# A decode kernel that streams a key and value cache: four accumulated products, other cuts of the loads, no marking loads

## The chip, the cores and the metric

The kernel runs on one core of a Trainium2 chip. A core has five engines that run side by side: TensorE (PE, matrix products into PSUM), VectorE (DVE), ScalarE (ACT), GpSimd (POOL) and SyncE (SP, which here only issues transfers). Sixteen DMA engines move data between HBM and the on-chip memory SBUF. The metric is the device time of one execution in microseconds.

## The reference

Two blocks share a normalised input and are added to it. Block A is one decode step of attention with 32 heads, 4 batches and a cache of 4096 positions of 128 numbers. Block B is a small gated unit (a projection to 1728, GELU, a layer norm of one half, a gate, a projection back to 640). In essence:

```
xn = layernorm(x)                               # x is (4, 1, 640)
q = (xn @ wq) as (4, 32, 1, 128)
p = softmax(q . k_cache * 128 ** -0.5)          # k_cache, v_cache: (4, 32, 4096, 128), bf16
A = (p . v_cache) as (4, 1, 4096) @ wo          # wo is (4096, 640)
z = gelu(xn @ w_in); z1, z2 = halves of z; z2 = layernorm(z2)
out = x + A + (z1 * (w_sp * z2 + b_sp)) @ w_out
```

Nearly all bytes are the two caches, 134 MB each, and each is read once.

## The kernel before

**Units.** The 32 heads are taken in four groups of eight (`g`), and within a group the four batches (`b`) one after another. A unit is the K or the V cache of one group and batch: 128 partitions by 64 KB, 8 MB. There are 16 K units (K0 to K15) and 16 V units; unit number u is group u // 4, batch u % 4. A partition holds 256 positions of one head, 16 partitions make a head.

**Order.** `seq` (L153) is K0, K1, K2, K3, then V0, K4, V1, K5 and so on to V11, K15, then V12 to V15. The main loop (L553) first issues the load of the next unit on SP's queue and then emits the work of the present one. SP's queue is served in order, so a load that waits holds back those behind it. A framework adds the waits between engines and may place instructions of one engine in another order than the text.

**Slots.** `kv` (L94) has five slots of 32 KB in each partition, and a unit takes two. `place` (L159 to L166) says which: V units lie in slots 0 and 1, even K units in 3 and 4, odd ones in 2 and 3 (there are other places at the start; V13 lies in 2 and 3, V15 in 3 and 4). A load waits until what lay in its slots has been consumed. `cuts` (L167) lists units that are loaded in pieces: K3, K7, K11 and K15 (the last of each group) in two halves, and V15 as 192 and 64 of its 256 positions. `first` (L169) lists K units of which the second half is consumed first: the odd ones from u = 4 that are not cut (K5, K9, K13). That half of an odd unit lies in slot 3, which the next unit needs.

**A K unit** (`emit_K`, L409) is eight steps: DVE transposes a piece (L417), PE multiplies it with q into the scores S (L428). After the last unit of a group, `softmax` (L469) finds the largest score (L435 to L445), takes the exponential on ACT (L473), transposes it on DVE (L479) and spreads it (`z_fill`, L448) over ACT, DVE and POOL into two buffers of weights, for batches 0 and 1.

**A V unit** (`emit_V`, L492) is 64 products (L500) into O. DVE masks and sums O into R (L509, L510; for V15 in four steps, L512 and L514). For batches 0 and 1, `z_fill` for the batch two later follows.

**The heads of a group.** `emit_sel` and `emit_oT` turn R (partitions by batch by 128 numbers) into rows of oT, the stationary operand of the last projection. One f32 product with SelX spreads the heads over 32 rows (L523), where every row holds all four quarters of its head's 128 numbers. DVE masks the quarter that belongs to the row (L526), adds the four (L537) and multiplies by the inverse row sum (L538). For groups one to three this stands inside the last K unit of the next group, for group four at the end.

**The end.** `load_wo` (L193) loads wo into slots 0 and 1 (40 KB in each partition, 32 columns of 640) in pieces of 16, 11, 4 and 1 columns. The products of columns 0 to 15 (L546; CL is 16) are added to `proj` in PSUM, which already holds x and block B; DVE copies and adds its halves (L587, L591) while PE does columns 16 to 31 into `last`. L601 adds both and two transfers write the result.

**The start.** wq, w_in, pieces of w_out and K0 are loaded; POOL and DVE build constant masks (SelX among them, L259) and block B is computed while K0 and K1 arrive. Six small loads into the tile `walk` (L557 to L559) follow on SP's queue; nothing reads them. They are the marking loads: each has its own size and row count, by which it can be told in a list of transfers.

Of the kernel before, what the change touches and what calls it, by code (L numbers as in the profile page):

```python
# [9 lines left out]
ALU = mybir.AluOpType  # L10
AX = mybir.AxisListType
F32 = mybir.dt.float32
BF16 = mybir.dt.bfloat16
# [3 lines left out]
def kernel(  # L17
# [19 lines left out]
    nc = tc.nc  # L37
    P = 128
    B, Sq, D = A_x.shape
# [3 lines left out]
    HG = 8  # L43
# [3 lines left out]
    T = Sk // M  # L47
# [5 lines left out]
    NU = NG * B  # L53
# [21 lines left out]
    const = ctx.enter_context(tc.tile_pool(name="const", bufs=1))  # L75
    small = ctx.enter_context(tc.tile_pool(name="small", bufs=2))

    NKT = 2 * TC * 32
    ppool = ctx.enter_context(tc.tile_pool(name="ppool", bufs=2))
# [8 lines left out]
    def misc_ps(shape, dtype):  # L88
        misc_ctr[0] += 1
        return ps_m.tile(shape, dtype, tag="misc", name=f"misc{misc_ctr[0]}")  # L90
# [38 lines left out]
    w_in = at_slot(2, n_in).rearrange("p (c f) -> p c f", c=DC)  # L129
    nc.sync.dma_start(out=w_in, in_=B_w_in.rearrange("(p c) f -> p c f", c=DC))  # L130

    walk = const.tile([8, 286], BF16)
    sw = nc.gpsimd.dma_start(out=walk[:, 0:128], in_=B_w_out[0:8, 0:128].rearrange("(r i) n -> i r n", i=4))
    MS = 15 * NOUT // 2
    nc.vector.memset(w_words[:, 0:MS], 0.0)
    nc.gpsimd.memset(w_words[:, MS:FC * NOUT // 2], 0.0)
# [2 lines left out]
    def load_piece(eng, t):  # L139
        p0, p1, st, c0, n, k, run = PC[t]  # L140
        return eng.dma_start(out=w_out[p0:p1:st, c0:c0 + n].rearrange("p c n -> p (c n)"),
                             in_=B_w_out[f_of[t][0]:f_of[t][1], :].rearrange("(r i c) n -> i r (c n)", i=k, c=run))
# [3 lines left out]
    for t in ("w", "s", "n", "m", "l"):  # L146
        with tc.issue_after(sw.ins):
            sw = load_piece(nc.gpsimd, t)
# [10 lines left out]
    place = {("k", 0): (3, 4), ("k", 1): (0, 1), ("k", 2): (2, 3), ("k", 3): (4, 0)}  # L159
# [2 lines left out]
    for u in range(NU):  # L162
        place[("v", u)] = (0, 1)
    place[("v", 0)] = (1, 2)
    place[("v", NU - 3)] = (2, 3)
    place[("v", NU - 1)] = (3, 4)  # L166
    cuts = {("k", u): (0, T // 2, T) for u in range(NU) if u % B == B - 1}  # L167
    cuts[("v", NU - 1)] = (0, 192, T)
    first = {u: u % 2 for u in range(B, NU) if ("k", u) not in cuts}  # L169

# [18 lines left out]
    CW = H * Dh // P  # L189
    RQ = Dh // CW  # L190
    wo_t = at_slot(0, CW * NOUT).rearrange("p (c n) -> p c n", c=CW)

    def load_wo(c_cuts):  # L193
        for c0, c1 in zip(c_cuts[:-1], c_cuts[1:]):
            nc.sync.dma_start(out=wo_t[:, c0:c1, :], in_=A_wo.rearrange("(p c) n -> p c n", c=CW)[:, c0:c1, :])
# [55 lines left out]
    SelH = const.tile([P, HG], F32)  # L251
    i2 = SelP[:].rearrange("p (h c) -> p c h", c=2)
    nc.gpsimd.tensor_tensor(out=SelH[:], in0=i2[:, 0], in1=i2[:, 1], op=ALU.add)
    Mk4 = const.tile([P, 4], F32)
# [1 line left out]
    nc.gpsimd.tensor_tensor(out=h4[:, 0:16], in0=I32[:, 0:16], in1=I32[:, 16:32], op=ALU.add)  # L256
    nc.gpsimd.tensor_tensor(out=h4[:, 16:24], in0=h4[:, 0:8], in1=h4[:, 8:16], op=ALU.add)
    nc.gpsimd.tensor_tensor(out=Mk4[:], in0=h4[:, 16:20], in1=h4[:, 20:24], op=ALU.add)
    SelX = const.tile([P, HG, RQ], F32)  # L259
    nc.gpsimd.tensor_copy(out=SelX[:], in_=SelH[:, :, None].to_broadcast((P, HG, RQ)))  # L260
    MkB = const.tile([P, B], F32)
    b8 = const.tile([P, 8 + HP], F32)
    nc.gpsimd.tensor_tensor(out=b8[:, 0:8], in0=SelP[:, 0:8], in1=SelP[:, 8:16], op=ALU.add)
# [5 lines left out]
    for q in range(4):  # L269
        nc.gpsimd.tensor_copy(out=SelE[32 * q:32 * q + 32, :, q % 2, :],  # L270
                              in_=b8[32 * q:32 * q + 32, 8:8 + HP, None].to_broadcast((32, HP, RQ)))
# [10 lines left out]
                          in_=ident_f[:].rearrange("p (q x c) -> p q x c", q=2, c=C2))  # L282
# [4 lines left out]
    for hf in range(NH):  # L287
        nc.tensor.matmul(proj[0:32, 0:NO2], lhsT=ident_bf[:XR, 1 - hf:33 - hf],  # L288
                         rhs=x_bf[:, hf * NO2:(hf + 1) * NO2], start=(hf == 0), stop=False)
# [4 lines left out]
    for hf in range(2):  # L294
        for c in range(DC):
            for j in range(NG):
                n0 = j * HG * Dh + hf * 512
                nc.tensor.matmul(q4_ps[32 * j:32 * j + 32, hf * 512:hf * 512 + 512], lhsT=xnT[:, c, :],  # L298
                                 rhs=wq[:, c, n0:n0 + 512], start=(c == 0), stop=(c == DC - 1))
# [4 lines left out]
    for a in range(2):  # L304
        op = nc.vector.tensor_copy if a == 0 else nc.scalar.copy
# [34 lines left out]
    for c in range(DC):  # L340
        for parts in z_parts:
            for j, (dst, src) in enumerate(parts):
                nc.tensor.matmul(dst, lhsT=xnT[:, c, :], rhs=src[:, c], start=(c == 0 and j == 0),  # L343
                                 stop=(c == DC - 1 and j == len(parts) - 1))
# [4 lines left out]
    for (bk, q, t), (col, m, n, c0, x0, x1, st) in z_at_col.items():  # L349
        rows = slice(32 * q, 32 * q + 32)  # L350
        nc.scalar.activation(out=zT[rows, :, c0:c0 + n, x0:x1:st],  # L351
                             in_=zr_ps[bk][rows, :, col:col + m].rearrange("p a (x c) -> p a c x", c=n),
# [37 lines left out]
    for f0 in range(0, FC, 4):  # L390
        for hf in range(NH):
            for fc in range(f0, min(f0 + 4, FC)):
                nb = 32 if fc == 1 and hf == 0 else RW
                u0, r0 = 32 * fc + 1 - hf, 32 * (fc % 2)
                nc.tensor.matmul(proj[r0:r0 + nb, 0:NO2], lhsT=uT[:, u0:u0 + nb],  # L395
                                 rhs=w_out[:, fc, hf * NO2:(hf + 1) * NO2],
                                 start=(fc == 1 and hf == 0), stop=False)
# [9 lines left out]
    state = {}  # L407
# [110 lines left out]

    def emit_sel(g):

        ox = misc_ps([P, B, RQ, CW], F32)
        r0 = 32 * g
        nc.tensor.matmul(ox[r0:r0 + 32].rearrange("p b q c -> p (b q c)"), lhsT=SelX[:].rearrange("p h q -> p (h q)"),  # L523
                         rhs=state["R"][:].rearrange("p b d -> p (b d)"), start=True, stop=True)
        om = ppool.tile([P, B, RQ, CW], F32, tag="p", name="om")
        nc.vector.tensor_tensor(out=om[r0:r0 + 32], in0=ox[r0:r0 + 32],  # L526
                                in1=Mk4[r0:r0 + 32, None, :, None].to_broadcast((32, B, RQ, CW)), op=ALU.mult)
        state[("om", g)] = om

    oT = const.tile([P, CW * RW + 32], BF16)  # L530
    nc.gpsimd.memset(oT[:], 0.0)

    def emit_oT(g):
        r0 = 32 * g
        om = state.pop(("om", g))
        oR = small.tile([P, B, CW], F32, tag="oR", bufs=1)
        nc.vector.tensor_reduce(out=oR[r0:r0 + 32], in_=om[r0:r0 + 32].rearrange("p b q c -> p b c q"), axis=AX.X, op=ALU.add)  # L537
        nc.vector.tensor_tensor(out=oT[r0:r0 + 32, 1:1 + CW * RW].rearrange("p (c b h) -> p c b h", c=CW, h=NH)[:, :, :, 0],  # L538
                                in0=oR[r0:r0 + 32].rearrange("p b c -> p c b"),
                                in1=state.pop(("rinv", g))[r0:r0 + 32, None, :].to_broadcast((32, CW, B)), op=ALU.mult)  # L540

    def o_mul(dst, c, hf, n0, n1, start, stop):
# [10 lines left out]
    for i, item in enumerate(seq):  # L553
        if i + 1 < len(seq):
            key, u = seq[i + 1]
            load_unit(seq[i + 1])
            if i == 0:  # L557
                for k, m0, m in ((1, 128, 72), (2, 200, 56), (8, 256, 24), (1, 280, 2), (1, 282, 2), (1, 284, 2)):
                    nc.sync.dma_start(out=walk[0:k, m0:m0 + m], in_=B_w_out[0:k, 0:m])  # L559
        else:  # L560
            load_wo((0, 16, 27, 31, 32))
        key, u = item
        g, b = divmod(u, B)
        if key == "k":
            done = b == B - 1 and g > 0
            for k in range(8):
                emit_K(u, k)
                if done and k == 1:
                    emit_sel(g - 1)
                if done and k == 2:  # L570
                    emit_oT(g - 1)
            if b == B - 1:
                if g < NG - 1:
                    fill_qz(g + 1)
                softmax(g)
        else:
            emit_V(u)
    emit_sel(NG - 1)
    emit_oT(NG - 1)

    CL = 16
    for c in range(0, CL, 2):
        for hf in range(NH):
            for p in range(2):
                o_mul(proj[32 * p:32 * p + 32], c + p, hf, hf * NO2, (hf + 1) * NO2, False, c == CL - 2 and hf == NH - 1)
    o_1 = ppool.tile([32, NO2], F32, tag="p", name="o_1")
# [3 lines left out]
    for k in range(2):  # L590
        nc.vector.tensor_tensor(out=o_q[32 * k:32 * k + 32, :], in0=proj[32:64, k * NQ:(k + 1) * NQ],  # L591
                                in1=o_1[:, k * NQ:(k + 1) * NQ], op=ALU.add)
    last = ps_l.tile([64, NQ], F32)
    for c in range(CL, CW):
        for hf in range(NH):
            for k in range(2):
                n0 = hf * NO2 + k * NQ
                o_mul(last[32 * k:32 * k + 32], c, hf, n0, n0 + NQ, c == CL and hf == 0, c == CW - 1 and hf == NH - 1)

# [33 lines left out]
```

## Time and profile before

| what | value |
|---|---|
| median of three runs | 663.61 us (662.76 to 663.67) |
| the profiled execution | 663.03 us |
| its span (first to last instruction) | 661.1 us |
| HBM read | 282.25 MB, 427 GB/s over the span |
| DVE busy | 378.3 us, 57% (283.0 of it the transposes of L417) |
| PE busy | 286.1 us, 43% |
| ACT, POOL busy | 74.7 and 76.6 us |
| the chain that ended last | DMA 72%, issue 12%, DVE 10%, PE 4% |

The profile is that of one execution. It gives the busy time of each engine, the busy share in 40 slices (a digit 9 is 90% or more), the chain of work that ended last (at each step, what released it), and a timeline: start, duration, engine, line, operation, output and input, how many, and in brackets the idle time before and what ended it. The span is 1.9 us shorter than the time of the same execution. A line L417 is a line of the kernel before.

### The profile page before, as it was taken

The numbers are of one execution on the slowest core, as the hardware profiler recorded it, in microseconds if no ns is written. First come the engines' busy times: TensorE is split into PE (matmuls) and PEld (weight loads), VectorE is DVE, ScalarE is ACT, GpSimd is POOL, SyncE is SP. The second block draws the span as 40 slices with busy tenths as digits, with TensorE's granted clock in tenths as the row PEclk, the third lists the DMA queues.
The fourth block names the chain that finished last, engine by engine and source line by source line (L and its number), as shares of the span: only waits on it lengthen the run. The fifth ranks groups of instructions, "written<-read, shape, count | busy, mean of one in ns | idle before, by whom it ended". The sixth has DMA issues, their size and how long they took to land.

```text
span 661.1 us, 5628 instructions
## 1 busy us (share of the span) xinstructions
PE 286.1 (43%) x2345; PEld 107.8 (16%) x2345; DVE 378.3 (57%) x312; ACT 74.7 (11%) x144; POOL 76.6 (12%) x135
## 2 busy tenths in 40 slices
PE   0436556336062546315335165533517065632145
PEld 0222212112021111101112021111202021111013
DVE  4239999756191759719164377756537195870112
ACT  0310000331100000430200000060200000061100
POOL 7440000031200000030300000030300000021200
PEclk9858888769578596667768587766857667865678
DMA  9999999999999999999999999999999999999997
GB/s 368 446 447 433 409 445 424 444 441 428 429 428 433 444 407 450 425 433 440 441 416 433 432 420 453 440 417 441 421 436 440 437 428 415 434 438 436 420 423 297
DMA packets 6686, 282.60 MB, mean 427 GB/s; under 512 B 1096, under 2 KB 1232, under 8 KB 1364
## 3 DMA queue, kind: packets, MB, share of 16 engines
q1 hardware_dynamic: 6266, 281.60, 98.8%
q0 software_dynamic: 368, 0.65, 0.3%
q8 instruction: 18, 0.29, 0.2%
q14 instruction: 6, 0.05, 0.0%
q10 hardware_dynamic: 28, 0.01, 0.0%
HBM read 282.25 MB, written 0.01 MB: 427 GB/s over the span
## 4 chain that ended last, share of the span: by engine, by line
DMA 72%; issue 12%; DVE 10%; PE 4%; POOL 1%; ACT 1%; SPq 0%; DVEq 0%; POOLq 0%; ACTq 0%
DMA kv<-in_A_k_cache_dram 54%; DMA kv<-in_A_v_cache_dram 10%; DVE w_words L417 10%; DMA kv<-in_A_wo_dram 4%; DMA kv<-in_B_w_in_dram 4%; PE O L500 2%; PE proj L395 1%; POOL kv L379 0%; PE misc L343 0%; PE S L428 0%; PE last L546 0%; ACT kv L351 0%; POOL z_b L381 0%; POOL kv L364 0%; ACT L351 0%
## 5 line engine op out<-in xcount | busy, mean ns | idle before, releaser
L417 DVE STREAM_TRANSPOSE w_words<-kv 128x2048 f32<-128x2048 f32 x128 | 283.0, 2276 | 118.3 <-DMA kv<-in_A_k_cache_dram 115.8
L428 PE MATMUL S<-w_words,QZ 128*32 128x512 bf16 x1024 | 183.9, 491 | 253.8 <-DVE w_words L417 253.8
L428 PEld LDWEIGHTS <-QZ 128*32 128x32 bf16 x1024 | 59.2, 109 | 377.7 <-issue 312.9
L500 PE MATMUL O<-kv,w_words 128*32 128x512 bf16 x1024 | 74.8, 457 | 55.7 <-DMA kv<-in_A_v_cache_dram 48.2
L465 ACT ACTIVATE w_words<-w_words,MkE 32x128 bf16<-32x128 bf16 x120 | 60.8, 507 | 115.0 <-PE O L500 101.9
L509 DVE TENSOR_TENSOR om<-O,Mk 128x512 f32<-128x512 f32 x15 | 10.4, 692 | 91.0 <-PE O L500 91.0
L463 POOL TENSOR_SCALAR w_words<-w_words,MkE 32x128 bf16<-32x128 bf16 x60 | 43.1, 719 | 136.3 <-PE O L500 115.3
L500 PEld LDWEIGHTS <-w_words 128*32 128x32 bf16 x1024 | 33.8, 112 | 96.6 <-issue 65.6
L473 ACT ACTIVATE w_words<-S,negmax 128x1024 bf16<-128x1024 f32 x4 | 4.5, 1114 | 396.6 <-DVE negmax L445 396.6
L403 POOL COPY QZ<-qT 32x32 bf16<-32x32 bf16 x16 | 5.1, 317 | 268.0 <-PE S L428 267.5
L461 DVE TENSOR_SCALAR w_words<-w_words,MkE 32x128 bf16<-32x128 bf16 x76 | 24.9, 327 | 2.4
L510 DVE TENSOR_REDUCE R<-om 128x128 f32<-128x512 f32 x15 | 15.3, 1019 | 0.5
L484 POOL TENSOR_SCALAR rs<-MkB,rowsum 128x4 f32<-128x4 f32 x4 | 1.2, 299 | 112.7 <-ACT w_words L473 112.7
L479 DVE STREAM_TRANSPOSE w_words<-w_words 128x1024 bf16<-128x1024 bf16 (+1 forms) x8 | 9.6, 1241 | 5.9 <-ACT w_words L473 5.9
L395 PE MATMUL proj<-w_words,z_b 128*8 128x320 bf16 (+1 forms) x52 | 5.9, 411 | 8.8 <-DVE z_b L382 8.8
L512 DVE TENSOR_SCALAR R<-O,Mk 128x128 f32<-128x128 f32 x1 | 0.4, 352 | 14.0 <-PE O L500 14.0
L435 DVE TENSOR_REDUCE m<-S 128x1 f32<-128x1024 f32 x4 | 4.9, 1225 | 5.6 <-PE S L428 5.6
L523 PE MATMUL misc<-R,SelX 128*32 128x512 f32 x8 | 4.2, 604 | 7.2 <-DVE R L510 5.5
L298 PE MATMUL q<-kv,xnT 128*32 128x512 bf16 x40 | 4.1, 590 | 6.2 <-DVE xnT L228 6.2
L487 PE MATMUL misc<-rs,SelE 128*32 128x4 f32 x8 | 1.1, 205 | 10.7 <-POOL rs L484 10.7
L288 PE MATMUL proj<-kv,ident_bf 8*32 8x320 bf16 x2 | 0.7, 445 | 10.8 <-DMA kv<-in_A_x_dram 10.8
L526 DVE TENSOR_TENSOR om<-misc,Mk 32x512 f32<-32x512 f32 x4 | 2.7, 687 | 4.5 <-PE misc L523 4.5
(101 smaller groups left out, 92.9 us busy)
## 6 DMA issues: line engine op xcount, KB each, us to landing
kv<-in_A_k_cache_dram SPq DMA_DIRECT2D x8, 4096.0 KB, 29.8
kv<-in_A_v_cache_dram SPq DMA_DIRECT2D x1, 6144.0 KB
kv<-in_A_wq_dram SPq DMA_DIRECT2D x1, 5120.0 KB
kv<-in_A_wo_dram SPq DMA_DIRECT2D x1, 2560.0 KB
kv<-in_B_w_in_dram SPq DMA_DIRECT2D x1, 2160.0 KB, 23.7
kv<-in_A_v_cache_dram SPq DMA_DIRECT2D x1, 2048.0 KB
kv<-in_A_wo_dram SPq DMA_DIRECT2D x1, 1760.0 KB
kv<-in_A_wo_dram SPq DMA_DIRECT2D x1, 640.0 KB, 26.7
```

Source lines behind the costliest of these rows:

```text
L395: nc.tensor.matmul(proj[r0:r0 + nb, 0:NO2], lhsT=uT[:, u0:u0 + nb], rhs=w_out[:, fc, hf * NO2:(hf + 1) * NO2], start=(fc == 1 and hf == 0) ...
L403: nc.gpsimd.tensor_copy(out=QZ[r0:r0 + 32, :, :, :, 8 + 8 * hp], in_=qT[32 * g:32 * g + 32, NE * hp:NE * hp + NE].rearrange("p e a b -> p ...
L417: nc.vector.transpose(kT.rearrange("p (t r) -> p t r", r=32), kw)
L428: nc.tensor.matmul(S_ps[32 * q:32 * q + 32, i], lhsT=QZ[:, b, 2 * kh + w, e, w0:w0 + 32], rhs=kb[:, i, :, e, :, w], start=(b == 0 and k < ...
L435: nc.vector.tensor_reduce(out=m1[:], in_=S_ps[:].rearrange("p i t m -> p (i t m)"), axis=AX.X, op=ALU.max)
L461: nc.vector.tensor_scalar(out=dst, in0=src, scalar1=mk, scalar2=None, op0=ALU.mult)
L463: nc.gpsimd.tensor_scalar(out=dst, in0=src, scalar1=mk, scalar2=None, op0=ALU.mult)
L465: nc.scalar.activation(out=dst, in_=src, func=ACT.Copy, scale=mk)
L479: nc.vector.transpose(pT_t[:, j0:j1, :], blocks)
L500: nc.tensor.matmul(O_ps[32 * q:32 * q + 32, :, :], lhsT=Zb[b % 2][:, w].rearrange("p h c -> p (h c)"), rhs=vv[:, w * 4 * Dh:(w + 1) * 4 * ...
L509: nc.vector.tensor_tensor(out=om4[:], in0=O_ps[:], in1=Mk4[:, :, None].to_broadcast((P, 4, Dh)), op=ALU.mult)
L510: nc.vector.tensor_reduce(out=R, in_=om4[:].rearrange("p c d -> p d c"), axis=AX.X, op=ALU.add)
```

## The change

- `emit_sel` makes four accumulated products instead of one. SelX becomes four blocks, one for each quarter d of the 128 numbers; block d sends head h to the row of quarter d alone. The sum of the four products is what L526 and L537 made on DVE, and these two go.
- wo is loaded in pieces of 12, 8, 8, 3 and 1 columns, and columns 0 to 19 go into `proj` (CL is 20).
- K7, K11 and K15 are loaded whole; K3 alone stays in two halves. By the rule of `first`, their second halves are then consumed first.
- V13 lies in slots 3 and 4, V15 in 2 and 3.
- The six marking loads go, and `walk` shrinks to what the one GpSimd load needs.

```diff
-    walk = const.tile([8, 286], BF16)
+    walk = const.tile([8, 128], BF16)
...
-    place[("v", NU - 3)] = (2, 3)
-    place[("v", NU - 1)] = (3, 4)
-    cuts = {("k", u): (0, T // 2, T) for u in range(NU) if u % B == B - 1}
+    place[("v", NU - 3)] = (3, 4)
+    place[("v", NU - 1)] = (2, 3)
+    cuts = {("k", B - 1): (0, T // 2, T)}
...
-    SelX = const.tile([P, HG, RQ], F32)
-    nc.gpsimd.tensor_copy(out=SelX[:], in_=SelH[:, :, None].to_broadcast((P, HG, RQ)))
+    SelX = const.tile([P, RQ, HG * RQ], F32)
+    nc.gpsimd.memset(SelX[:].rearrange("p d r -> p (d r)"), 0.0)
+    sx = SelX[:]
+    nc.gpsimd.tensor_copy(out=bass.AP(sx.tensor, sx.offset, [list(sx.ap[0]), [HG * RQ + 1, RQ], [RQ, HG]]),
+                          in_=SelH[:, None, :].to_broadcast((P, RQ, HG)))
...
-        ox = misc_ps([P, B, RQ, CW], F32)
+        ox = misc_ps([P, B, CW], F32)
         r0 = 32 * g
-        nc.tensor.matmul(ox[r0:r0 + 32].rearrange("p b q c -> p (b q c)"), lhsT=SelX[:].rearrange("p h q -> p (h q)"),
-                         rhs=state["R"][:].rearrange("p b d -> p (b d)"), start=True, stop=True)
-        om = ppool.tile([P, B, RQ, CW], F32, tag="p", name="om")
-        nc.vector.tensor_tensor(out=om[r0:r0 + 32], in0=ox[r0:r0 + 32],
-                                in1=Mk4[r0:r0 + 32, None, :, None].to_broadcast((32, B, RQ, CW)), op=ALU.mult)
-        state[("om", g)] = om
+        for d in range(RQ):
+            nc.tensor.matmul(ox[r0:r0 + 32], lhsT=SelX[:, d], rhs=state["R"][:, :, d * CW:(d + 1) * CW],
+                             start=(d == 0), stop=(d == RQ - 1))
+        state[("ox", g)] = ox
...
-        om = state.pop(("om", g))
-        oR = small.tile([P, B, CW], F32, tag="oR", bufs=1)
-        nc.vector.tensor_reduce(out=oR[r0:r0 + 32], in_=om[r0:r0 + 32].rearrange("p b q c -> p b c q"), axis=AX.X, op=ALU.add)
         nc.vector.tensor_tensor(out=oT[r0:r0 + 32, 1:1 + CW * RW].rearrange("p (c b h) -> p c b h", c=CW, h=NH)[:, :, :, 0],
-                                in0=oR[r0:r0 + 32].rearrange("p b c -> p c b"),
+                                in0=state.pop(("ox", g))[r0:r0 + 32].rearrange("p b c -> p c b"),
                                 in1=state.pop(("rinv", g))[r0:r0 + 32, None, :].to_broadcast((32, CW, B)), op=ALU.mult)
...
-            if i == 0:
-                for k, m0, m in ((1, 128, 72), (2, 200, 56), (8, 256, 24), (1, 280, 2), (1, 282, 2), (1, 284, 2)):
-                    nc.sync.dma_start(out=walk[0:k, m0:m0 + m], in_=B_w_out[0:k, 0:m])
         else:
-            load_wo((0, 16, 27, 31, 32))
+            load_wo((0, 12, 20, 28, 31, 32))
...
-    CL = 16
+    CL = 20
```

More of the change, by code (lines that the diff above doesn't have):

```diff
@@ L130 @@
     nc.sync.dma_start(out=w_in, in_=B_w_in.rearrange("(p c) f -> p c f", c=DC))
-    walk = const.tile([8, 286], BF16)
-    sw = nc.gpsimd.dma_start(out=walk[:, 0:128], in_=B_w_out[0:8, 0:128].rearrange("(r i) n -> i r n", i=4))
+    walk = const.tile([8, 128], BF16)
+    sw = nc.gpsimd.dma_start(out=walk[:], in_=B_w_out[0:8, 0:128].rearrange("(r i) n -> i r n", i=4))
     MS = 15 * NOUT // 2
```

## The prediction

> **What bounds the kernel now.** I read the busy slices first, then the chain, then two stretches of the timeline (the end of group two, the end of the program), then the clock by stages.
>
> ```profile
> DMA  9999999999999999999999999999999999999997
> HBM read 282.25 MB, written 0.01 MB: 427 GB/s over the span
> ```
>
> The DMA engines are never idle before the last slice. So a part of the change counts only if it alters the transfers themselves, lets the queue run dry, or lies behind the last landing. The chain (start, duration, what) gives the price of a cut:
>
> ```profile
> 344.48 29.75 DMA kv<-in_A_k_cache_dram
> ...
> 383.18 29.84 DMA kv<-in_A_k_cache_dram
> ...
> 422.05 29.67 DMA kv<-in_A_k_cache_dram
> ...
> 630.26 25.50 DMA kv<-in_A_wo_dram
> ...
> 655.80 2.56 PE last L546 x64
> ```
>
> Start plus duration is a landing: 374.23, 413.02, 451.72. Each interval holds one V and one K unit. The second (38.70) has both whole, the first (38.79) has K11 in two halves: a cut costs **0.09 us**. The last two lines say that the products into `last` start when the wo piece of columns 16 to 26 has landed (655.76).
>
> The end of group two, and the same work at the end of group one, where no transfer is waited for:
>
> ```profile
> 64.41 17.66 DVE L417 STREAM_TRANSPOSE w_words<-kv 128x2048 f32<-128x2048 f32 x8 [0.17 <-DMA kv<-in_A_k_cache_dram]
> 83.76 35.20 DVE L417 STREAM_TRANSPOSE w_words<-kv 128x2048 f32<-128x2048 f32 x16 [1.69 <-DMA kv<-in_A_k_cache_dram]
> 128.77 6.22 PE L500 MATMUL O<-kv,w_words 128*32 128x512 bf16 x64 [3.55 <-ACT w_words L465]
> ...
> 258.05 8.89 DVE L417 STREAM_TRANSPOSE w_words<-kv 128x2048 f32<-128x2048 f32 x4 [0.92 <-DMA kv<-in_A_k_cache_dram]
> 266.97 0.33 SPq L186 DMA_DIRECT2D kv<-in_A_k_cache_dram  x1
> 277.68 5.11 PE L500 MATMUL O<-kv,w_words 128*32 128x512 bf16 x64 [4.25 <-DMA kv<-in_A_v_cache_dram]
> 282.83 0.33 SPq L186 DMA_DIRECT2D kv<-in_A_v_cache_dram  x1
> ```
>
> Four transposes of K7's second half, then the load of K8; later V4's products, and at their end the load of V5. A unit's eight transposes take 17.66 us. From the last transpose of group one (118.96) to V0's first product are 9.81 us. The end of the program, and the clock in its stages (the number before "DMA share" is the granted clock, the second-last pair DMA share and GB/s):
>
> ```profile
> 648.49 1.04 PE L523 MATMUL misc<-R,SelX 128*32 128x512 f32 x2 [1.62 <-DVE R L514]
> 649.57 0.70 DVE L526 TENSOR_TENSOR om<-misc,Mk 32x512 f32<-32x512 f32 x1 [1.14 <-PE misc L523]
> 650.30 1.01 DVE L537 TENSOR_REDUCE oR<-om 32x128 f32<-32x512 f32 x1
> 651.35 0.37 DVE L538 TENSOR_TENSOR oT<-oR,rinv 32x128 bf16<-32x128 f32 x1
> 651.78 3.52 PE L546 MATMUL proj<-kv,oT 128*8 128x320 bf16 x32 [2.24 <-DVE oT L538]
> ```
>
> ```profile
> 645.93:649.34 3.41, 1.79 (x21) 0.36 (x10) 1.40 (x4) 0.00 (x0) 0.00 (x0) 1.00 0.98 417
> 649.34:652.76 3.42, 1.18 (x17) 0.67 (x18) 2.08 (x3) 0.00 (x0) 0.00 (x0) 1.00 0.97 407
> 652.76:656.17 3.41, 2.91 (x27) 1.55 (x25) 0.79 (x2) 0.00 (x0) 0.00 (x0) 0.50 0.95 394
> 656.17:659.58 3.41, 2.18 (x62) 1.97 (x57) 0.64 (x3) 0.00 (x0) 0.00 (x0) 1.00 0.11 41
> ```
>
> The head step (L523 to L538) ends at 651.72, the 32 products into `proj` at 655.30, and the 64 into `last` find the clock full. PE was busy 1.18 us in the second stretch, and the clock of the third is half; 2.91 us in the third, and the fourth is full.
>
> **The change, part by part.** Sums are against the profiled execution (663.03 us: span 661.1 and 1.9 around it), which is 0.58 under the median of the runs shown, 663.61.
>
> *K7, K11, K15 whole.* Three cuts less on the path that bounds: 3 x -0.09 = **-0.27**. What it moves: each of these loads now waits for slot 3, until four transposes of the K unit before it are done; that is when its second half was issued (228.10 for K7). V3 ahead of it lands at 238.5, so 10 us are spare; V4's load behind it on SP's queue waits for PE until 242.32 in either form. The unit is now consumed second half first, so slot 3 is free after four transposes (266.97, as now) and K8 is issued as now. But all eight transposes follow the landing: 258.05 + 17.66 = 275.71 instead of 266.94, so softmax is 8.8 us later. V4's first product: 275.71 + 9.81 = 285.5 instead of 277.68; at 6.22 for 64 its last is at 291.7, and V5's load is issued then instead of at 282.83. That is a longer wait in SP's queue; behind it stands K9's load, which waits for DVE until 305.78 anyway. The queue holds K8 until 296.84. From issue to landing the 5 KB output takes 1.43 us (658.73 to SP's end of wait at 660.16), so the load has to be issued by 295.4: **3.7 us are spare, cost 0**. The same sum for V9 (K11's transposes begin at 413.13; 6.5 us for V8's products; K12 lands at 451.72) leaves 3.2, for V14 (568.04; V13 lands at 606.6) 3.5. Behind on PE are K8's products (K8 lands at 296.84). On DVE V4's two operations end at 293.5, before K8's transposes at 296.86; the z_fill on POOL (6.36 us) ends near 298, and V6 lands behind K9 (335.54). If this cover is gone, each us past it costs one us at each of three places.
>
> *V13 to slots 3, 4 and V15 to 2, 3.* V13's load needs four transposes of K15 (568.04 + 8.89 = 576.93; it is issued at 576.96 now). V15 needs V13's products as now (612.9), and slot 2, which K15 leaves at 585.7. The wo slots are those of V14 as now. Cost 0.
>
> *wo in five pieces.* One cut more: **+0.09**.
>
> *No marking loads.* Six loads of 1 to 8 short rows less. On SP they wait for wq to land while K1's load behind them waits for qT (24.80), with K0 in the queue until past 40: 0 there. On the DMA engines a load of 128 rows costs 0.09, so theirs is between 0 and 6 x 0.09 = 0.54; few rows make it nearer to 0: **-0.05**. DMA in sum: **-0.23**.
>
> *SelX.* A memset of 128x128 and a wider copy on POOL during the set-up, at most 0.6 together (the QZ memset of 128x640 takes 0.62). POOL is done at 22.4 and waits for DVE until 24.51: hidden. If it were not, qT and K1's load would be late, and K0 would still cover them.
>
> *Heads of O.* DVE loses L526 and L537: 0.70 + 1.01 and two gaps of 0.04 = -1.79. PE: one f32 product (a pair of instructions, 512 columns, 1.04) becomes four of 128 columns. Bounds: the same 1024 streamed columns, 1.04; or four times the 128-column pair of L439 (0.49), 1.96. I take 1.25, nearer to the first, since nothing is read between them: +0.21. In groups one to three DVE waits for a K landing behind it (0.91 to 0.92 us idle), so the gain there is 0. In the last group oT is done at 651.72 - 1.58 - 0.23 = 649.9.
>
> *CL = 20.* Forty products into `proj` instead of 32: from 649.9, with columns 12 to 19 landing near 652.9 (655.76 - 7 x 0.39 - 0.23 + 0.09; 0.39 a column follows from 655.76 and the landing of columns 27 to 30 at 657.34). At 0.11 (3.52 / 32) the last 16 end at 654.7, the DVE sums after them (0.48 and 0.65) by 656, off the path. `last` now has 48 products, its first 32 at columns 20 to 27, which land at 655.76 + 0.39 - 0.23 = 655.92. At full clock (2.56 / 64 = 0.04 each) they end at 657.2; columns 28 to 30 have landed (657.1), twelve more end at 657.7, four more at **657.85**. Now it is 658.36. So **-0.5** in all, the DMA's -0.23 included. At half clock, 0.08 each, it is 655.92 + 48 x 0.08 = 659.8, +1.4.
>
> [...]
>
> **The rivals.**
>
> 1. *The queue runs dry after V4, V8 and V12* (slower). Place: the loads of V5, V9 and V14 on SP. For it: PE's 64 products vary with the clock (5.11 to 6.22), and the 16 engines do not drain together, so the first may be idle before 296.84. Against: over 3 us of cover, and the engine that ends last decides. It decides from 4 us more than the sum; 1 us beyond the cover three times gives 663.1 + 3 = 666.1.
> 2. *The last products meet the half clock.* The forty products begin earlier and wait for wo in the middle, so PE is less busy in the stretch before `last`: 16 products after 652.9 at 0.11 (3.52 / 32) or less are at most 1.8 us, and of the rows above 1.18 us was followed by the half clock, 1.79 by the full. Against: before runs the same risk with 64. +1.4: 664.4, within 0.2% of the median.
> 3. *A load has a fixed cost that the queue does not hide.* K and wo make two loads less net. At the 1.43 us of the output load that is -2.9: 663.61 - 2.9 = 660.7. Against: 38.79 and 38.70, 0.09 a cut. [...]
>
> **How the numbers follow.** A measurement of this kernel can tell about 0.2% (1.3 us) from no change. Forecast: 663.61 - 0.5 = **663.1**, chance 0.62, own range 662.3 to 664.0 (marking loads at -0.54; the runs shown spread by 0.9). Rival 2: 0.20. Rival 1: 0.12. Rival 3: 0.04. Anything else 0.02. Within 0.2%: forecast and rival 2, less a little at the edges, 0.80. Faster: rival 3 and part of the rest, 0.06. Slower: rival 1, the edge of rival 2, 0.14. The range, 662.2 to 665.0, takes in rival 2 and the first stalls of rival 1.
>
> **What would show it.** Right: DMA slices full up to the last; intervals between K landings 38.70 everywhere after group one; V5's load issued near 291.5 without a gap in the K landings; oT near 650; `last` ending 0.1 to 0.4 us behind the last wo landing. Wrong: a K or V interval above 19.4 per unit at 296, 451 or 606 (rival 1); 48 products into `last` in 3.5 us or more (rival 2); a last landing more than 1 us earlier (rival 3).

## The result and the profile after

The changed kernel takes 665.25 us (median of six runs, 664.66 to 665.91); the kernel before, beside it, 662.79 (six runs, 662.64 to 663.67). The ratio is **1.0035 [1.0024, 1.0046]**: slower, by the ratio 2.3 us, where 663.1 and no change were forecast. The profiled execution of the changed kernel is its second fastest run: 664.68 us, span 662.8, so 1.65 us behind the profiled execution of before.

The page of the changed kernel, the busy share of the DMA engines in 40 slices and the total:

```profile
DMA  9999999999999999999999999999999999999996
HBM read 282.25 MB, written 0.01 MB: 426 GB/s over the span
```

By this view nothing has happened: in every slice but the last the engines are over 90% busy. The cause is below its resolution (a slice is 16.6 us).

The end of group two, in the timeline (start, duration, engine, line, operation, count, idle time before and what ended it):

```profile
257.77 17.66 DVE L420 STREAM_TRANSPOSE w_words<-kv 128x2048 f32<-128x2048 f32 x8 [12.37 <-DMA kv<-in_A_k_cache_dram]
266.69 0.33 SPq L186 DMA_DIRECT2D kv<-in_A_k_cache_dram  x1
286.31 5.65 PE L503 MATMUL O<-kv,w_words 128*32 128x512 bf16 x64 [3.83 <-DVE w_words L464]
292.00 0.33 SPq L186 DMA_DIRECT2D kv<-in_A_v_cache_dram  x1
296.49 17.66 DVE L420 STREAM_TRANSPOSE w_words<-kv 128x2048 f32<-128x2048 f32 x8 [2.73 <-DMA kv<-in_A_k_cache_dram]
```

All eight transposes follow K7's landing, K8 is issued after four of them, V4's products end at 291.96 and V5's load goes out at 292.00 (forecast 291.7). The forecast of the order is right. So the question is what a load issued 4.5 us before K8's landing (296.46) costs. In the landings of this one execution it costs nothing at once: from the transposes of K8 (296.49) to those of K9 (335.20) are 38.71 us, before 38.70.

The end of the program, in the timeline, and the clock of its stages (the row's pairs are busy us and count of PE, weight loads, DVE, ACT and POOL, then the granted clock, the DMA share and GB/s):

```profile
648.30 1.06 PE L527 MATMUL misc<-R,SelX 128*32 128x128 f32 x8 [1.61 <-DVE R L517]
649.40 0.31 DVE L536 TENSOR_TENSOR oT<-misc,rinv 32x128 bf16<-32x128 f32 x1 [1.15 <-PE misc L527]
650.43 1.80 PE L544 MATMUL proj<-kv,oT 128*8 128x320 bf16 x24 [1.07 <-DMA kv<-in_A_wo_dram]
653.53 1.26 PE L544 MATMUL proj<-kv,oT 128*8 128x320 bf16 x16 [1.29 <-DMA kv<-in_A_wo_dram]
656.62 3.39 PE L544 MATMUL last<-kv,oT 128*32 128x160 bf16 x48 [1.84 <-DMA kv<-in_A_wo_dram]
```

```profile
648.84:652.25 3.41, 2.32 (x29) 1.48 (x28) 0.31 (x1) 0.00 (x0) 0.00 (x0) 1.00 1.00 419
652.25:655.66 3.41, 1.26 (x16) 0.77 (x16) 0.79 (x2) 0.00 (x0) 0.00 (x0) 1.00 0.99 411
655.66:659.08 3.42, 2.46 (x38) 2.46 (x39) 0.32 (x1) 0.00 (x0) 0.00 (x0) 0.50 0.28 106
```

The head step is done at 649.71, 2.0 us earlier than before. Then PE waits for wo twice and is busy only 1.26 of 3.41 us in the second stretch; the third has half the clock, and the 48 products into `last` take 3.39 us. Two terms can be read off against the forecast of 655.92 to 657.85 for them: they start 0.7 us late (656.62) and take 1.46 us longer (3.39 for 1.93). So this one execution lost mostly by the clock. It is no proof for the median, which lies 0.6 higher; the runs below had to divide that.

The completion records of the transfers in the trace give one more reading. There are 16 of them for a load, one for the share of each DMA engine. In the kernel before those of K8 came at 293.45 (the first), 295.07 (the mean) and 296.84 (the last): the engines ended this load 3.4 us apart.

### The profile page after: what moved, and what is told of

Read it like the earlier page. It is cut to its first block, busy times and chain, and to the rows that moved or that the text cites. A ratio compares the mean times of both kernels' runs of the same rounds, so it can differ in the third digit from the quotient of the medians.

```text
span 662.8 us, 5648 instructions
## 1 busy us (share of the span) xinstructions
PE 291.6 (44%) x2361; PEld 112.0 (17%) x2361; DVE 371.6 (56%) x304; ACT 74.8 (11%) x144; POOL 76.4 (12%) x136
## 4 chain that ended last, share of the span: by engine, by line
DMA 69%; DVE 12%; issue 12%; PE 4%; POOL 1%; ACT 1%; SPq 0%; DVEq 0%; POOLq 0%; ACTq 0%
DMA kv<-in_A_k_cache_dram 58%; DVE w_words L420 11%; DMA kv<-in_A_wo_dram 4%; DMA kv<-in_A_v_cache_dram 4%; DMA kv<-in_B_w_in_dram 4%; PE O L503 2%; PE proj L398 1%; PE last L544 1%; POOL kv L382 0%; PE misc L346 0%; ACT kv L354 0%; DVE w_words L482 0%; PE S L431 0%; POOL z_b L384 0%; DVE w_words L464 0%
## 5 line engine op out<-in xcount | busy, mean ns | idle before, releaser
L431 PE MATMUL S<-w_words,QZ 128*32 128x512 bf16 x1024 | 187.9, 500 | 259.6 <-DVE w_words L420 259.6
L503 PE MATMUL O<-kv,w_words 128*32 128x512 bf16 x1024 | 76.3, 463 | 44.3 <-DMA kv<-in_A_v_cache_dram 29.1
L512 DVE TENSOR_TENSOR om<-O,Mk 128x512 f32<-128x512 f32 x15 | 10.4, 692 | 82.7 <-PE O L503 82.6
L527 PE MATMUL misc<-R,SelX 128*32 128x128 f32 x32 | 4.2, 276 | 7.2 <-DVE R L513 5.5
L544 PEld LDWEIGHTS <-oT 128*8 128x8 bf16 (+1 forms) x88 | 5.0, 109 | 5.5 <-issue 4.2
```

The lines of the kernel that those rows point to most:

```text
L431: nc.tensor.matmul(S_ps[32 * q:32 * q + 32, i], lhsT=QZ[:, b, 2 * kh + w, e, w0:w0 + 32], rhs=kb[:, i, :, e, :, w], start=(b == 0 and k < ...
L503: nc.tensor.matmul(O_ps[32 * q:32 * q + 32, :, :], lhsT=Zb[b % 2][:, w].rearrange("p h c -> p (h c)"), rhs=vv[:, w * 4 * Dh:(w + 1) * 4 * ...
L512: nc.vector.tensor_tensor(out=om4[:], in0=O_ps[:], in1=Mk4[:, :, None].to_broadcast((P, 4, Dh)), op=ALU.mult)
L544: nc.tensor.matmul(dst[0:nb, 0:n1 - n0], lhsT=oT[:, c0:c0 + nb], rhs=wo_t[:, c, n0:n1], start=start, stop=stop)
```

## The experiments

**Theory L (late load).** V5's load (and V9's, V14's) comes when the first engines have already run out of work; they lose their lead, and the slowest engine ends later. **Theory C (clock).** `last` meets the half clock more often, because the forty products are done in pieces between the landings. **Theory U (unit).** A K unit in one piece, or its other slots, costs something by itself, wherever V5's load stands. **Theory M (marks).** The loads that go changed something at the start. L and C are the rivals 1 and 2 of the prediction. All kernels were timed against the kernel before on the same chip; three comparisons hold four kernels each: first the four parts alone; then K whole with V in halves, K7 whole, both parts of the end, and the change without its K part; last the two with late loads and the two with PE kept busy. The kernel before had 662.81 us in the first (27 runs), 662.80 in the second (33), 663.60 in the third (28), so only ratios go across.

**One part alone, four kernels.** Only the marking loads go:

```diff
-    walk = const.tile([8, 286], BF16)
+    walk = const.tile([8, 128], BF16)
...
-            if i == 0:
-                for k, m0, m in ((1, 128, 72), (2, 200, 56), (8, 256, 24), (1, 280, 2), (1, 282, 2), (1, 284, 2)):
-                    nc.sync.dma_start(out=walk[0:k, m0:m0 + m], in_=B_w_out[0:k, 0:m])
```

> The kernel before without the six marking loads, nothing else changed. Clock theory (the last products into `last` meet the half clock because PE is idle between the wo pieces): within 0.2 us of before, since the end of the program is untouched. Dry-queue theory (V5, V9, V14 are loaded too late because K7, K11, K15 come whole): 0 as well. Marking-loads theory (without them the load of each DMA engine or the waits of the first K loads change): +1 to +2.4 us, and the last landing of wo is later than 657.7.

663.32 us (663.12 to 663.94), ratio 1.0009 [1.0000, 1.0018]. Slightly slower, at the edge of what can be told. In its profiled execution (663.15) the last piece of wo landed at 657.56, as in before (657.67), and the `last` products end at 658.07 (658.35): the half microsecond is not seen there, and its cause stays open.

Only wo in five pieces:

```diff
-            load_wo((0, 16, 27, 31, 32))
+            load_wo((0, 12, 20, 28, 31, 32))
...
-    CL = 16
+    CL = 20
```

> The kernel before with wo in pieces of 12, 8, 8, 3, 1 columns and 40 products into `proj`, 48 into `last`; heads of O still by one product and two DVE operations. Clock theory: the forty products begin at 651.7, when columns 12 to 19 are about to land, so PE has no gap within them and is idle only from about 655 on; `last` meets the full clock in most runs and ends near 657.9: -0.4 to +0.5 us against before. If the wo cuts alone cost the clock, +1.2 us or more. Dry-queue and marking-loads theories: within 0.3 us.

662.89 us (662.77 to 663.45), ratio 1.0001 [0.9992, 1.0010]. Timeline of its end:

```profile
651.58 4.56 PE L546 MATMUL proj<-kv,oT 128*8 128x320 bf16 x40 [2.23 <-DVE oT L538]
656.16 1.90 PE L546 MATMUL last<-kv,oT 128*32 128x160 bf16 x48
```

With the old head step oT is late enough for the forty products to run without a gap; the clock is full for `last` (1.90 for 48; the granted clock from 655.66 to 659.08 was 0.97).

Only the four accumulated products (the hunks of SelX, `emit_sel` and `emit_oT` of the change; SelX's other layout with them):

```diff
-        nc.tensor.matmul(ox[r0:r0 + 32].rearrange("p b q c -> p (b q c)"), lhsT=SelX[:].rearrange("p h q -> p (h q)"),
-                         rhs=state["R"][:].rearrange("p b d -> p (b d)"), start=True, stop=True)
...
+        for d in range(RQ):
+            nc.tensor.matmul(ox[r0:r0 + 32], lhsT=SelX[:, d], rhs=state["R"][:, :, d * CW:(d + 1) * CW],
+                             start=(d == 0), stop=(d == RQ - 1))
```

> The kernel before with the heads of O by four accumulated products, wo in its old pieces. Clock theory: oT is ready near 650, before columns 0 to 15 land at 651.5; the 32 products run from 651.5 to about 654, and PE is then idle until 655.76, so the stretch before `last` may be too idle: the 64 products take 2.5 us at the full clock (then -0.1 us against before) or 5 us at the half clock (then +2.4 us), mixed over the runs. Dry-queue and marking-loads theories: within 0.3 us.

662.75 us (662.54 to 663.33), ratio 0.9998 [0.9989, 1.0007]. Its end:

```profile
648.93 0.31 DVE L536 TENSOR_TENSOR oT<-misc,rinv 32x128 bf16<-32x128 f32 x1 [1.15 <-PE misc L527]
651.70 3.71 PE L544 MATMUL proj<-kv,oT 128*8 128x320 bf16 x32 [2.81 <-DMA kv<-in_A_wo_dram]
```

oT is ready at 649.24, but the first piece of wo (16 columns) lands at 651.7: the gain on DVE turns into a wait.

Only K7, K11 and K15 whole, with the slots of V13 and V15:

```diff
-    place[("v", NU - 3)] = (2, 3)
-    place[("v", NU - 1)] = (3, 4)
-    cuts = {("k", u): (0, T // 2, T) for u in range(NU) if u % B == B - 1}
+    place[("v", NU - 3)] = (3, 4)
+    place[("v", NU - 1)] = (2, 3)
+    cuts = {("k", B - 1): (0, T // 2, T)}
```

> The kernel before with K7, K11, K15 whole and V13 and V15 in each other's slots. Clock theory: -0.3 us (three cuts less), the end of the program as before. Dry-queue theory: +1 to +2.4 us, and an interval between unit landings above 19.4 us behind V4, V8 or V12. Marking-loads theory: -0.3 us.

664.67 us (five runs, 664.04 to 666.87), ratio **1.0036 [1.0022, 1.0050]**: by itself as much as the whole change. Its timeline near the second place (V9's load, then K12's and K13's transposes):

```profile
446.27 0.33 SPq L186 DMA_DIRECT2D kv<-in_A_v_cache_dram  x1
451.26 17.66 DVE L417 STREAM_TRANSPOSE w_words<-kv 128x2048 f32<-128x2048 f32 x8 [3.23 <-DMA kv<-in_A_k_cache_dram]
491.47 4.51 DVE L417 STREAM_TRANSPOSE w_words<-kv 128x2048 f32<-128x2048 f32 x2 [15.05 <-DMA kv<-in_A_k_cache_dram]
```

Transposes start 0.02 to 0.03 us behind a landing, so two such starts give the time of one V and one K unit. Before it was 451.75 to 490.46, 38.71; here 40.21, 1.5 more. L and U both give a longer interval, but the records of this trace show no engine without a packet at V9's load: all of the 1.5 us is one engine's, which took 20.87 us for K13, where the others took 19.35, and so became the last. The part on the prediction comes back to it.

**The late load mended, the unit kept whole.** V5, V9 and V14 come in halves, and the products of the first V unit of a group take one half of it after the other, so the first half of V5 can be issued earlier; K7, K11 and K15 stay whole, and V13 and V15 keep the slots of the change:

```diff
+    for u in (B + 1, 2 * B + 1, 3 * B + 2):
+        cuts[("v", u)] = (0, T // 2, T)
...
-        parts = [(qp, x) for x in range(C2) for qp in range(2)] if v == 0 else [(qp, x) for qp in range(2) for x in range(C2)]
+        parts = [(qp, x) for x in range(C2) for qp in range(2)] if b == 0 else [(qp, x) for qp in range(2) for x in range(C2)]
```

> K7, K11, K15 whole as in the change, but V5, V9 and V14 are loaded in two halves, and V4, V8, V12 take the products of their first slot first, so the first half of the next V unit is issued after 32 products instead of 64. Dry-queue theory (V5, V9, V14 issued at 292 and later cost the 1.9 us of the kernel with whole K units): the first halves are issued about 3 us earlier, no DMA engine goes idle, and the time is within 0.4 us of before. If whole K units cost in another way (the order of their halves, the 8.8 us later softmax): still +1.5 to +2.4 us.

662.86 us (662.54 to 663.59), ratio **1.0000 [0.9991, 1.0008]**: the loss is gone. Timeline at the first place:

```profile
285.75 6.42 PE L502 MATMUL O<-kv,w_words 128*32 128x512 bf16 x64 [3.82 <-DVE w_words L463]
289.48 3.06 SPq L188 DMA_DIRECT2D kv<-in_A_v_cache_dram  x2
```

V5's first half goes out at 289.48, 2.7 us before the end of V4's products. U falls for the whole unit and the slots; that the loss has to do with three more cuts could still be said.

**One place alone.** Only K7 whole:

```diff
-    cuts = {("k", u): (0, T // 2, T) for u in range(NU) if u % B == B - 1}
+    cuts = {("k", u): (0, T // 2, T) for u in range(NU) if u % B == B - 1 and u != 2 * B - 1}
```

> The kernel before with K7 alone whole; K11 and K15 in halves, V13 and V15 in their old slots. Dry-queue theory: one late load (V5 near 292) of three, +0.3 to +0.9 us. If only the last late load (V14) costs, or the swapped slots of V13 and V15: 0. If a single late load costs everything: +1.9 us.

663.99 us (663.10 to 664.95), ratio 1.0017 [1.0008, 1.0026]. In the profiled execution (664.95, its slowest) V4's products met the half clock (6.39 us from 286.93; granted 0.50 from 288.00 to 292.50), and V5's load went out at 293.36. Rows of 1.5, 1.5 and 2 us around it:

```profile
291.00:292.50 1.50, 1.50 (x20) 0.61 (x16) 0.62 (x2) 1.42 (x4) 1.32 (x3) 0.50 0.95 404
292.50:294.00 1.50, 0.82 (x16) 0.22 (x8) 0.63 (x1) 1.42 (x4) 1.32 (x3) 0.98 0.61 262
294.00:296.00 2.00, 0.00 (x0) 0.00 (x0) 1.08 (x2) 1.92 (x4) 1.82 (x3) 0.99 1.37 492
```

The DMA share falls to 0.61 for 1.5 us (packets are not cut at a row's edge, so a share can pass 1). V5's load comes 1.36 us later than with all three K units whole (292.00): V4's products start 0.62 us later (286.93 for 286.31 in the change) and take 0.74 us longer. So the moment of V5's load also hangs on the clock that the products before it happen to meet: the 64 took 5.11 us at a mean granted clock of 0.70 in before, 5.65 at 0.63 in the change, 6.39 here.

**Late without any change of K.** The kernel before, with products into a scratch tile of PSUM ahead of V4's; nothing reads it. Twenty of them, and forty-four:

```diff
+        if v == B:
+            fill = ps_s.tile([32, 512], F32, tag="S", name="fill")
+            for _ in range(20):
+                nc.tensor.matmul(fill[:], lhsT=Zb[b % 2][:, 0].rearrange("p h c -> p (h c)"), rhs=vv[:, 0:512], start=True, stop=True)
```

> The kernel before, K loads in halves, with 20 idle products on PE ahead of V4's 64 (a scratch result that nothing reads). They take 6 to 8.5 us by the clock, so V5's load is issued near 288 to 290 instead of 282.83. Dry-queue theory with a threshold near 291 (the first DMA engine runs out of K8 at 292.8, and a load needs more than 1 us from issue to its first bytes): 0, within 0.3 us. If every late V load costs in proportion: +0.7 us.

> The same with 44 idle products, 11 to 13 us: V5's load is issued near 292 to 294, as late as in the kernel with K7 whole or a little later, and nothing else differs from before. Dry-queue theory: +1 to +2.5 us from this one late load, with idle DMA engines near 293. If it was the whole K unit that cost and not the late load: 0.

Twenty: 663.57 us (662.54 to 664.45), ratio 0.9999 [0.9990, 1.0008]. Forty-four: 665.35 us (six runs, 664.63 to 667.10), ratio **1.0028 [1.0016, 1.0040]**. The timeline of twenty, V5's load and the transposes of K8 and K9:

```profile
287.12 0.33 SPq L186 DMA_DIRECT2D kv<-in_A_v_cache_dram  x1
...
296.61 17.66 DVE L417 STREAM_TRANSPOSE w_words<-kv 128x2048 f32<-128x2048 f32 x8 [7.73 <-DMA kv<-in_A_k_cache_dram]
335.31 11.08 DVE L417 STREAM_TRANSPOSE w_words<-kv 128x2048 f32<-128x2048 f32 x5 [13.55 <-DMA kv<-in_A_k_cache_dram]
```

and of forty-four:

```profile
293.22 0.33 SPq L186 DMA_DIRECT2D kv<-in_A_v_cache_dram  x1
...
296.72 17.66 DVE L417 STREAM_TRANSPOSE w_words<-kv 128x2048 f32<-128x2048 f32 x8 [1.74 <-DMA kv<-in_A_k_cache_dram]
336.10 11.08 DVE L417 STREAM_TRANSPOSE w_words<-kv 128x2048 f32<-128x2048 f32 x5 [11.92 <-DMA kv<-in_A_k_cache_dram]
```

One load 4.3 us later than the kernel before has it costs nothing (38.70 from K8 to K9); 10.4 us later it costs (39.38), with K in halves, V13 and V15 where they were and wo as it was. By the prediction's count this load was early enough too: 3.5 us before K8's landing (296.7), and 1.43 needed. That settles L against U.

The profiled executions side by side; idle is the time in which engines had no packet between 292 and 296 us, summed over the 16 engines, from the packet records; the third column is the last piece of wo:

| kernel | V5's load issued | idle engine time | last landing | ratio of the runs |
|---|---|---|---|---|
| before | 282.83 | none | 657.67 | 1 |
| twenty products | 287.12 | none | 657.45 | 0.9999 |
| K whole, V in halves | 289.48 (first half) | none | 657.52 | 1.0000 |
| the change mended (last run) | 290.58 (first half) | none | 657.68 | 1.0003 |
| K whole | 292.00 | 2.1 us | 658.60 | 1.0036 |
| the change | 292.00 | 1.05 us | 658.16 | 1.0035 |
| forty-four products | 293.22 | 6.5 us | 659.75 | 1.0028 |
| K7 whole | 293.36 | 7.1 us | 659.73 | 1.0017 |

The point from which V5's load costs lies between 290.6 and 292.0, not at 295.4. That fits the packet records: the first engine has no packet of K8 left from 292.8 on (292.83 in the change; 292.96 in before, where the first share is recorded complete at 293.45), and in the four traces with idle engines most of these got their first packet of V5 1.0 to 1.7 us behind its issue, so the load is due by 291.1 to 291.8, an estimate from these figures.

The same records say where the change loses nothing. V9 is issued at 446.32 and the first engine reports K12 complete at 449.06; V14 at 601.95, and the first engine is done with V13 at 604.97. Idle engine time there is 0.03 us and none in the change, none at either place with K whole. In these traces only V5 came too late. Whether V9 or V14 does in other executions, where the clock of the products before them is another, no trace shows; K whole costs more than K7 whole alone (0.36% and 0.17%), but their intervals overlap.

**Both parts of the end.** Four products and five pieces together, nothing else:

> Both parts of the change that touch the end of the program, alone: four accumulated products, wo in five pieces, 40 and 48 products; K loads in halves and marking loads as before. Clock theory: as in the changed kernel's profile, PE waits for wo before and within the 40 products, and the 48 into `last` meet the half clock (3.4 us instead of 1.9) in many runs: +0.5 to +1.3 us, though each part alone costs nothing. Dry-queue theory: within 0.3 us.

663.16 us (662.66 to 664.33), ratio 1.0005 [0.9996, 1.0014]. The eleven times are in two groups, six from 662.66 to 663.16 and five from 663.85 to 664.33. The profiled one (664.17) is of the second:

```profile
649.83 1.80 PE L544 MATMUL proj<-kv,oT 128*8 128x320 bf16 x24 [0.63 <-DMA kv<-in_A_wo_dram]
652.93 1.25 PE L544 MATMUL proj<-kv,oT 128*8 128x320 bf16 x16 [1.30 <-DMA kv<-in_A_wo_dram]
656.03 3.29 PE L544 MATMUL last<-kv,oT 128*32 128x160 bf16 x48 [1.84 <-DMA kv<-in_A_wo_dram]
```

```profile
652.25:655.66 3.41, 1.25 (x16) 0.76 (x16) 1.11 (x3) 0.00 (x0) 0.00 (x0) 1.00 0.97 405
655.66:659.08 3.42, 3.05 (x48) 3.04 (x47) 0.00 (x0) 0.00 (x0) 0.00 (x0) 0.50 0.25 93
```

The same 1.25 us of PE, the same half clock, 3.29 us. The full-clock price is 1.90 (five pieces alone), so 1.4 us, about the distance of the two groups (their medians are 1.3 apart).

Why one half of the executions? In the clock records the granted clock stands for 3.41 us or a multiple of it, and these stretches begin elsewhere in each trace (652.26 here, 651.69 in the next kernel's, 652.76 in before). The traces of before and of the change, cut into such stretches, have 167 at the full clock: the 65 with PE busy for less than 0.405 of the stretch were all followed by the half clock, the 95 with more than 0.456 all by the full one, and of the seven between five by the half. With the rows above, the stretch ahead of `last` stays below 0.44, within that gap, if it begins between about 651.4 and 652.9: 1.5 of 3.41 us. If every start is as likely, which was not shown, that is an estimate of 0.44 of the executions. It was five of eleven.

**The change without its K part** (halves of K and the old slots of V13 and V15 put back):

```diff
-    place[("v", NU - 3)] = (3, 4)
-    place[("v", NU - 1)] = (2, 3)
-    cuts = {("k", B - 1): (0, T // 2, T)}
+    place[("v", NU - 3)] = (2, 3)
+    place[("v", NU - 1)] = (3, 4)
+    cuts = {("k", u): (0, T // 2, T) for u in range(NU) if u % B == B - 1}
```

> The changed kernel with K7, K11 and K15 in halves again and V13, V15 in their old slots. Dry-queue theory: what is left is the marking loads (+0.5 measured alone) and the end of the program: +0.2 to +0.9 us. Clock theory: +0.5 to +1.8 us. If the parts only cost together: still +2.4 us.

663.29 us (662.87 to 664.55), ratio 1.0011 [1.0002, 1.0020], again in two groups (six up to 663.29, five from 664.05). The profiled one (664.55) has the half clock (0.50 from 655.66 to 659.08): `last` 3.38 us from 656.16. So of the 0.35% the K part makes about 0.24, and the end with the marks about 0.11; alone the K part had 0.36, so the shares add up only within the intervals.

**PE kept busy between the landings.** Four and seven products into a scratch tile that nothing reads, after columns 0 to 11 and 12 to 19, added to both parts of the end:

```diff
+        for _ in range({10: 4, 18: 7}.get(c, 0)):
+            nc.tensor.matmul(fill[:], lhsT=oT[:, 0:32], rhs=wo_t[:, c + 1, 0:512], start=True, stop=True)
```

> Heads and wo parts of the change on the kernel before, and 4 and 7 idle products (a scratch result that nothing reads) in the two gaps in which PE waits for wo. Clock theory: the stretch before `last` is now busy enough, the 48 products take 1.7 to 1.9 us in every run, the slow half of the runs (664.0 to 664.3) is gone and the median is 662.3 to 662.7. If the slow runs have another cause: still two groups, 662.7 and 664.1.

663.66 us (663.28 to 664.24), ratio 1.0001 [0.9993, 1.0010].

```profile
657.07 1.86 PE L544 MATMUL last<-kv,oT 128*32 128x160 bf16 x48 [0.34 <-DMA kv<-in_A_wo_dram]
```

```profile
652.25:655.66 3.41, 2.97 (x31) 1.61 (x26) 0.40 (x1) 0.00 (x0) 0.00 (x0) 1.00 0.96 400
655.66:659.08 3.42, 2.93 (x53) 2.02 (x51) 0.83 (x4) 0.00 (x0) 0.00 (x0) 1.00 0.27 104
```

2.97 us busy instead of 1.25, and the clock stays full: 1.86 us. This trace's own stretches begin at 650.31, 653.72 and 657.14; the second holds 2.83 us of PE and is followed by the full clock, where without the idle products it would hold about 1.3 (an estimate: the sixteen products and the start of `last`), which three other traces (1.25, 1.26 and 1.35) have followed by the half clock. That is one execution. The time shows less: here the kernel before itself spread from 662.63 to 664.21, and in this profiled execution one engine was late with V14 (last engine 626.81, mean 625.16; in the run without the idle products 625.77 and 625.11), so `last` began at 657.07. That the loss of 0.05% in the median is mended is not shown.

**The change with both mended:** V5, V9 and V14 in halves, PE kept busy (the two diffs above, added to the changed kernel).

> The changed kernel with both causes mended: V5, V9, V14 in two halves with the first slot's products first (no late load), and the idle products in the two gaps. Dry-queue and clock theories together: within 0.5 us of before, most likely 0 to -0.4 us plus what the missing marking loads cost (0 to 0.5). If something else in the change costs: +1 us or more.

663.77 us (663.04 to 664.05), ratio 1.0003 [0.9994, 1.0012]. In its profiled execution (663.04) V5's first half went out at 290.58, no engine was idle, `last` took 1.90 us (here the stretches lie so that it would have met the full clock without the idle products too: the one from 650.91 would hold about 2.1 us):

```profile
290.58 3.10 SPq L188 DMA_DIRECT2D kv<-in_A_v_cache_dram  x2
...
656.14 1.90 PE L546 MATMUL last<-kv,oT 128*32 128x160 bf16 x48 [0.33 <-DMA kv<-in_A_wo_dram]
```

The loss of 0.35% is gone, and nothing is won: this is the kernel before within the error, and no version tried beat it.

## Why the prediction was wrong

**The step that failed** is the cover of V5's load (and, by the same sum, of V9's and V14's): "The queue holds K8 until 296.84 ... so the load has to be issued by 295.4: 3.7 us are spare, cost 0", with its reason in rival 1, "the engine that ends last decides". 296.84 is when the last engine reports its share; the first does at 293.45. A load issued at 292.0 finds engines without work (1.05 us summed in the change, 2.1 with K whole, 7.1 with K7 whole). With the load due by 291.1 to 291.8, V5's spare time was -0.9 to -0.2 us instead of 3.7. For V9 and V14 the sum had the same fault, but in the trace their cover held (0.03 us idle and none): K12's first engine is 2.7 us behind V9's issue, V13's 3.0 behind V14's, K8's 1.3 behind V5's. The cost measured with that part alone is 0.36% [0.22, 0.50]; V5 late by itself, with K in halves, costs 0.28% [0.16, 0.40].

**Why lost lead is not harmless.** Compare the last landing of wo by engine: K7 whole gives 656.54, 657.69, 659.73 (first, mean, last), before 655.98, 656.96, 657.67. The mean lost 0.7 us, the last 2.1. With K whole it is 0.1 and 0.9. From the records of before a unit takes an engine 19.35 us, but about 20.9 for one engine when an instruction fetch falls into the unit (18 packets of 16 KB on that queue, 0.95 to 1.10 us each, 0.2% of the DMA time). Read so, an engine ahead of the others has a reserve: if the engine that a fetch hits has a lead of more than the 1.5 us between the two, the landing does not move; if it is among the last, the landing is late. From V5 on the last engine's units took more than 0.5 us above 19.35, summed, in one of the ten traces without idle engines (PE kept busy, 0.97 at V14) and in all four with them (the change 0.6, K whole 1.5, K7 whole and forty-four products 2.4 each). With K whole the 1.5 is the fetch at 474.93, in K13. It fell on one of two engines that the packet records cannot tell apart, and one of the two had stood without a packet from 293.88 to 295.33. The moment of the load was varied in the runs; the fetches were not. So it is shown that the late load costs; how 0.1 to 0.9 us of mean delay become 0.5 to 2.1 us at the end is argued from records, not shown.

**Rival 1** was priced right in its mechanism and wrong in its bound: it decides from the forecast issue time itself, not "from 4 us more than the sum". Its 0.12 was far too low; its 666.1 is above the median of 665.25. Its sign, a longer interval of the landings at 296, hardly shows in the changed kernel (38.71): the loss comes later in the stream.

**Rival 2** happened, with the size given (1.46 us in the profiled execution, forecast +1.4) and for the reason given: few busy microseconds before `last`. Its chance of 0.20 was low: about half of the executions with both parts of the end are in the upper group (five of eleven, twice), as the estimate from the stretches gives. Neither part alone does it: with the old head step the forty products have no gap, with the old pieces the thirty-two begin late enough. The prediction had all the rows for it: 16 products at most 1.8 us, and 1.18 us followed by the half clock.

**The gain of the end** (-0.5) did not appear. Four products alone and five pieces alone are within 0.1% of before; also the lower group of both (from 662.66) is not below the kernel before (from 662.51).

**Right** were V5's, V9's and V14's issue (292.00, 446.32 and 601.95; forecast 291.7, 447.1 and 601.7), the head step (1.06 us for the products, bounds 1.04 to 1.96; oT at 649.71, forecast 649.9), and that a cut costs little, against rival 3: one load more for wo is 1.0001 [0.9992, 1.0010], which leaves no room for 1.43 us, and fewer loads made nothing faster. The 0.09 itself is too small for these runs. **The marking loads** were set at -0.05; alone they gave +0.5 us, [0, 1.2], and why is open.

## What to carry to other kernels

In this stream of loads, which bounds the kernel, V5's load was early enough only when its first packets started before the first DMA engine ran out (292.8), not the last: issued by 290.58 it cost nothing, from 292.00 on it cost, and its first packets came 1.0 to 1.7 us behind the issue. The landing that the profile shows is that of the last engine (296.84), so look at the spread of the completions (here 3.4 us) before calling a wait hidden. A slot's release that moves from "early" to "just in time" is to be priced with the variation of what releases it, here 64 products (5.65 us at a mean clock of 0.63, 6.39 with 0.50 for most of them). And finishing work earlier just to wait for pieces of a transfer lowered the clock of the products behind the wait here: 1.25 us of PE in the stretch of 3.41, then a clock of 0.50 and 3.29 us for 48 products that took 1.90 at the full clock.

## What the runs showed of the hardware

- In before the 16 engines ended K8 3.4 us apart (293.45 to 296.84), and at the end of the program they were still 1.7 us apart (655.98 to 657.67). A unit took an engine 19.35 us, and about 1.5 us more on the one engine on which an instruction fetch fell (20.9; the fetch itself 0.95 to 1.10).
- After the dry moment with K7 whole the engines that restart together (294.3 to 294.7) took 2.9 to 3.45 us for their first packets of 64 KB, and in the change those that got V5's first packets from 293.14 to 293.69 took 2.74 to 2.96; the median of these packets in before is 2.42. So the loss was more than the idle time.
- A full-clock stretch of 3.41 us with PE busy for 1.25, 1.26 and 1.35 us (0.37 to 0.40; both parts of the end, the change, the change without its K part) was followed by half the clock; with 2.83 us (PE kept busy between the landings) by the full clock. In the traces of before and of the change, 65 of 65 full-clock stretches below 0.405 were followed by the half clock and 95 of 95 above 0.456 by the full; after the half clock, 126 of 126 stretches below 0.766 were followed by the half clock and 62 of 62 above 0.827 by the full.
